# The head of an attention stage rearranged: clears, gate copies, a first sigmoid and the order of its loads

## The chip, the core and the metric

The kernel runs on one core of a Trainium2 chip. The metric is the device time of one execution in microseconds (us), lower is better. The core has five instruction queues that matter here, each working strictly in the order in which the program issues to it: PE (TensorE, matrix products), DVE (VectorE), ACT (ScalarE), POOL (GpSimd) and SP, which issues most of the loads. Some loads are issued from ACT's queue.

## What is computed

A gated linear attention over 4 batches, 8 heads, 768 positions of width 40, followed by two feed-forward layers: one in which 3072 tokens are routed to 8 experts, and one with a product of two projections. Only the first stage is touched by the change:

```python
for t in range(S):
    m_new = np.maximum(f_gate[:, :, t] + m, i_gate[:, :, t])
    f_stab = np.exp(f_gate[:, :, t] + m - m_new)
    i_stab = np.exp(i_gate[:, :, t] - m_new)
    m = m_new
    C = f_stab * C + i_stab * np.einsum('bhd,bhe->bhde', vt, kt)
    n = f_stab * n + i_stab * kt
    h_tilde = np.einsum('bhde,bhe->bhd', C, qt)
    denom = np.maximum(np.abs(np.einsum('bhd,bhd->bh', n, qt)), 1.0)
    o = 1.0 / (1.0 + np.exp(-o_gate[:, :, t]))
    y[:, :, t] = o * h_tilde / denom
```

(the indices that only broadcast are left out). All arithmetic is float32.

## The kernel before

The recurrence is computed in chunks of T = 128 positions. There are 6 chunks (`c`) and 4 batches (`b`), so 24 blocks, numbered `n = 4c + b`. All 8 heads of a block are worked on together.

**Per chunk**, `gates(c)` turns the gates of all batches and heads into exponents: a chain of small DVE operations on 128x128 tiles (a scan for the running maximum `mt`, then `lf`, `cc`, a second scan `A`, and `zs`), then three ACT operations (`hi`, and two parts of `EW`), then on DVE `ar` and `es1`, and from these the wide operands `mov` (8 heads, 128x1024) and `est` (4 batches, 128x512). `ar`, `es1` and `md` are small; `mov` and `est` are copies of `ar` and `es1` scaled by a 0/1 selector (`hsel`, `bsel`). For chunk 0 these copies are whole-tile multiplications, for later chunks they are twelve ACT copies spread through the blocks. `gates2(c)` transposes `EW` on PE (this needs the identity matrix `identf`) and brings the result to SBUF as `gt`.

**Per block**, `s1(n)` makes the weights `P` in two halves g: PE forms the exponents `pe` from `est` and `mov`, ACT takes `dd = exp(pe)`, POOL clears the upper triangle of `dd` (affine select), PE forms `pq` from `qr` (the loaded q and k), and DVE multiplies `P = pq * dd`. There is one `pe` buffer and there are two `pq` buffers. `s2(n)` multiplies by v on PE (`pv`, one buffer), updates the state (`pst`, `Cc`, `Cb`), and forms numerator `num` and denominator `den` on DVE. `xout(n)` multiplies `num` by 1/den and by the sigmoid of the output gate, `SG[c][:, b]`, on POOL, and stores the row. `s3` and `s4` feed the router.

**Buffers and loads.** `load(n)` issues five SP transfers: four of q and k into `qr[n % 3]` and one of v and k into `vk`. The `qr` tiles must be zero outside the loaded rows, so each of the three is cleared once before its first load. `load_o(c)` issues the transfer of the output gate (640 KB) from ACT's queue; `load_g(c)` that of the f and i gates (`fi`, 128 KB) from SP's.

**Order.** The schedule is written by hand: the program order of `attention` is the order of every queue. At the start: `consts` (POOL's `iota` of `jp`, then on DVE `identf` from it and the clear of `ones`), `load_g(0)` and the load of the selectors `gs`, the clears of `qr[0]`, `qr[2]`, `Cb` and two `xt` tiles on POOL and of `qr[1]` and `pst` on DVE, `load(0)`, `load(1)`, `load_o(0)`, then all of `gates(0)`, `load_g(1)`, `load_o(1)`, `gates2(0)`, `pre(0)`, `s1(0)`, then the clear and load of `wg`, and `consts2`. In `consts2` POOL's `iota` of `pcol` comes ahead of ACT's `thr`, which reads it, and DVE copies `thc` from `thr`. Then the loop over blocks runs: iteration `n` issues `load(n + 2)`, `s1(n + 1)` interleaved with `s2(n)`, and steps of a background generator (`fill`): from the start `gates(1)`, and from block 2 on the conversion of later weights. In iteration 0, behind the second half's matrix products of `s1(1)` and ahead of their DVE product `P`, stands `sig(0)`, the sigmoid of the first output gate: one ACT instruction over 128x1280 and a one-element exponential `warm` behind it. ACT holds the table of one set of functions at a time, and the profile shows a table load ahead of each of the two.

Of the kernel before, what the change touches and what calls it, by code (L numbers as in the profile page):

```python
# [14 lines left out]
AF = mybir.ActivationFunctionType  # L15
OP = mybir.AluOpType
# [4 lines left out]
B, H, S, D = 4, 8, 768, 40  # L21
T = 128
# [21 lines left out]
class Kern:  # L44
# [9 lines left out]
    def consts(self, es):  # L54
        nc, cp = self.nc, self.cp
        jp = self.jp = es.enter_context(self.tc.tile_pool(name="ajp", bufs=1)).tile([128, 128], F32, name="jp")
        nc.gpsimd.iota(jp, pattern=[[1, 128]], base=0, channel_multiplier=-1,
                       allow_small_or_imprecise_dtypes=True)
        self.identf = cp.tile([128, 128], F32, name="identf")
        nc.vector.tensor_scalar(self.identf, jp, 0.0, None, op0=OP.is_equal)  # L60
        self.spacer = cp.tile([1, 1], F32, name="spacer")
        self.ones = cp.tile([128, T], F32, name="ones")
        nc.vector.memset(self.ones, 1.0)

    def consts2(self):
        nc, cp, jp = self.nc, self.cp, self.jp
# [151 lines left out]
    def attention(self, es):  # L218
        tc, nc, a = self.tc, self.nc, self.a
# [9 lines left out]
        def load_g(c):  # L229
            t = ld.tile([128, 2, T], F32, name="fi", bufs=2)  # L230
            nc.sync.dma_start(t, a["fi4"][:, c])
            FI[c] = t
# [5 lines left out]
        hsel = gs[:, 6:14]  # L238
        dsel = gs[:, 14:30]
        psel = gs[:, 30:158]  # L240
        bsel = gs[:, 158:162]
# [3 lines left out]
        qr = [one.tile([128, 2 * H, T], F32, name=f"qr{i}") for i in range(NQ)]  # L245
        nc.gpsimd.memset(qr[0], 0.0)
        nc.vector.memset(qr[1], 0.0)
        nc.gpsimd.memset(qr[2], 0.0)
        Cb = one.tile([128, B, 4, 2, DE], F32, name="Cb")
        nc.gpsimd.memset(Cb, 0.0)  # L250
        Cc = one.tile([128, B, 4, DE], F32, name="Cc")
        xtb = [one.tile([128, 3, T], F32, name=f"xt{i}") for i in range(2)]
        for i in range(2):
            nc.gpsimd.memset(xtb[i][64:128, 2], 0.0)
        MT = {}
        pst = ps.tile([128, 4, DE], F32, name="pst")
        nc.vector.memset(pst, 0.0)
# [1 line left out]
        VK, SG, GA, PT, ST = {}, {}, {}, {}, {}  # L259

        def load(n):
            c, b = divmod(n, B)
            t = qr[n % NQ]
            bd = t[:, H:].rearrange("p (a s) t -> p a s t", s=2)
            for s in range(2):
                r, rs = slice(64 * s, 64 * s + D), slice(D * s, D * s + D)
                nc.sync.dma_start(t[r, 0:H], a["qk"][rs, c, b])
                nc.sync.dma_start(bd[r, :, s], a["qk"][rs, c, b, 0:4])
            v_ = ld.tile([128, H, DE + D], F32, name="vk")
            nc.sync.dma_start(v_, a["vk"][b, c])  # L270
            VK[n] = v_

        def load_o(c):
            o_ = ld.tile([128, B, DM], F32, name="og", bufs=2)
            SG[c] = o_
            self.dma(lambda: nc.scalar.dma_start(o_, a["og"][:, c]))

        def sig(c):
            nc.scalar.activation(SG[c], SG[c], AF.Sigmoid)
            nc.scalar.activation(warm, gs[0:1, 0:1], AF.Exp)  # L280

        def gates(c):
            t = FI.pop(c)
            fg, ig = t[:, 0], t[:, 1]
            mt = wk.tile([128, 1 + T], F32, name="mt")
            if c:
                nc.vector.tensor_copy(mt[:, 0:1], MT[c - 1][:, T:])
            else:
                nc.vector.memset(mt[:, 0:1], -1e30)
            MT[c] = mt  # L290
            mc, mp = mt[:, 1:], mt[:, 0:T]
            yield 0
            nc.vector.tensor_tensor_scan(mc, fg, ig, mp[:, 0:1], op0=OP.add, op1=OP.max)
            yield 0
            lf = wk.tile([128, T], F32, name="lf", bufs=1)
            nc.vector.tensor_add(lf, fg, mp)
            yield 0
            nc.vector.tensor_sub(lf, lf, mc)
            if c == 0:
                nc.vector.memset(lf[:, 0:1], 0.0)  # L300
            yield 0
            cc = wk.tile([128, T], F32, name="cc", bufs=1)
            nc.vector.tensor_sub(cc, ig, mc)
            A = wk.tile([128, T], F32, name="A", bufs=1)
            nc.vector.tensor_tensor_scan(A, self.ones, lf, 0.0, op0=OP.mult, op1=OP.add)
            yield 0
            zs = wk.tile([128, 2, T], F32, name="zs", bufs=1)
            nc.vector.tensor_scalar(zs[:, 1], A, za, oa, op0=OP.mult, op1=OP.add)
            nc.vector.tensor_sub(cc, cc, A)
            yield 0  # L310
            nc.vector.tensor_scalar(zs[:, 0], cc, zc, oc, op0=OP.mult, op1=OP.add)
            hi = wk.tile([128, 2, T], F32R, name="hi", bufs=1)
            EW = wk.tile([128, 2, T], F32, name="EW", bufs=1)

            def fin():
                nc.scalar.activation(hi, zs, AF.Copy)
                nc.scalar.activation(EW[:, 0], A, AF.Exp)
                nc.scalar.activation(EW[:, 1], cc, AF.Exp, bias=A[:, T - 1:T])

            yield from self.later(fin, False)  # L320
            ar = wk.tile([128, T], F32, name="ar", bufs=1)
            nc.vector.scalar_tensor_tensor(ar, hi[:, 1].bitcast(F32), b2, zs[:, 1], op0=OP.mult, op1=OP.add)
            mov = wk.tile([128, H, T], F32R, name="mov")

            def half(g):
                e = nc.vector if c == 0 and g else nc.gpsimd
                e.tensor_tensor(mov[:, 4 * g:4 * g + 4], ar[:, None, :].to_broadcast([128, 4, T]),
                                hsel[:, 4 * g:4 * g + 4, None].to_broadcast([128, 4, T]), op=OP.mult)

            if c == 0:  # L330
                half(0)
            es1 = wk.tile([128, T], F32, name="es1", bufs=1)
            nc.vector.scalar_tensor_tensor(es1, hi[:, 0].bitcast(F32), b1, zs[:, 0], op0=OP.mult, op1=OP.add)
            est = wk.tile([128, B, T], F32R, name="est")

            def spread(e, b0, b1_):
                e.tensor_tensor(est[:, b0:b1_], es1[:, None, :].to_broadcast([128, b1_ - b0, T]),
                                bsel[:, b0:b1_, None].to_broadcast([128, b1_ - b0, T]), op=OP.mult)

            if c == 0:  # L340
                spread(nc.vector, 0, 1)
            yield 0
            md = wk.tile([128, 16], F32, name="md", bufs=1)
            nc.vector.tensor_scalar(md, dsel, EW[:, 0, T - 1:T], None, op0=OP.mult)
            yield 0
            if c == 0:
                half(1)
                spread(nc.gpsimd, 1, B)
            else:
                def scaled(i0, i1):  # L350
                    for i in range(i0, i1):
                        if i < B:
                            nc.scalar.activation(est[:, i], es1, AF.Copy, scale=bsel[:, i:i + 1])
                        else:
                            nc.scalar.activation(mov[:, i - B], ar, AF.Copy, scale=hsel[:, i - B:i - B + 1])

                yield "w"
                for i in range(0, 12, 3):
                    scaled(i, i + 3)
                    yield "w"  # L360
            GA[c] = (est, mov, EW, md)
            yield 0
# [150 lines left out]
        def allof(g):  # L513
            for _ in g:
                pass

        NS = B * NC
        for n in range(2):
            load(n)
        load_o(0)  # L520
        self.hold = False
        allof(gates(0))
        load_g(1)
        load_o(1)
        gates2(0)
        pre(0)
        allof(s1(0))
        nc.vector.memset(wg, 0.0)
        nc.sync.dma_start(wg[:, 0:2, 0:E], a["moe_w_gate"][0:256, :].rearrange("(c p) e -> p c e", p=128))
        nc.sync.dma_start(wg[0:64, 2, 0:E], a["moe_w_gate"][256:320, :])  # L530
        self.consts2()
        self.hold = True
        bg.insert(0, gates(1))
        load_g(2)
        for n in range(NS):
            c, b = divmod(n, B)
            if n == 2:
                bg.append(m2)
            if True:
# [4 lines left out]
                if b == 3 and c + 1 < NC:  # L544
                    gates2(c + 1)
                    if c + 2 < NC:
                        bg.insert(0, gates(c + 2))
                        if c + 3 < NC:
                            load_g(c + 3)
                m = s1(n + 1) if n + 1 < NS else iter(())  # L550
                next(m, None)
                g = s2g(n)
# [4 lines left out]
                if n == 0:  # L557
                    sig(0)
                if b == 3 and c + 1 < NC:
                    sig(c + 1)  # L560
# [6 lines left out]
                g = s2(n)  # L567
# [662 lines left out]
```

## Time and profile before

| | us |
|---|---|
| median of 3 runs | 909.09 |
| lowest and highest of these | 905.57, 910.00 |
| the profiled execution, its own time | 908.33 |
| its span in the profile | 906.6 |
| PE busy | 822.6 |
| DVE busy | 538.4 |
| POOL busy | 415.9 |
| ACT busy | 353.3 |

The profiled execution lies 0.76 us under the median, and its span 1.7 us under its own time. Mean granted clock of TensorE in it: 0.955 of full speed. The attention takes the first 200 us or so of the span, the routing and the two feed-forward layers the rest. A row of a timeline gives start, duration, engine, line, operation, output and inputs with their shapes, and in brackets the idle time of the engine before it with what ended it.

### The profile page before, as it was taken

Reading aid. Unit: us, or ns where it says so; the run is one execution under the profiler, and the core shown is the slowest. Engines: PE = TensorE matmul, PEld = TensorE weight load, DVE = VectorE, ACT = ScalarE, POOL = GpSimd, SP = SyncE. Lnnn points to the kernel's source line nnn. Section 1 sums busy time; section 2 is a strip of 40 time slices with the busy share of each in tenths; the row PEclk is TensorE's granted clock in tenths of the full one; section 3 lists DMA queues with packets and bytes.
Section 4 is the critical chain, followed back from the end, with each engine's and each line's share of the span. In section 5 each row is a group of like instructions: output and inputs, shape, how many; then the busy total and the mean of one; then the engine's idle time right before and its main releaser. Section 6 shows DMA issues by size and latency. Waiting matters only on the chain.

```text
span 906.6 us, 15898 instructions
## 1 busy us (share of the span) xinstructions
PE 822.6 (91%) x5939; PEld 780.7 (86%) x5939; DVE 538.4 (59%) x1188; ACT 353.3 (39%) x720; POOL 415.9 (46%) x441
## 2 busy tenths in 40 slices
PE   4889889976888799989989999999999999999996
PEld 3778788875777799979879998999899999999996
DVE  7678898756866974776576687476764212311211
ACT  4778777610443332232233234224322532532321
POOL 5577787621513670464056338233723823532122
PEclk9999999995889989979989999999999999999999
DMA  6877777413122310220120122031111301200000
GB/s 169 245 230 213 234 214 228 136 59 104 52 67 81 89 59 9 76 75 22 54 80 18 37 78 59 1 97 48 30 53 45 105 24 44 76 1 23 1 1 22
DMA packets 51037, 73.84 MB, mean 81 GB/s; under 512 B 6160, under 2 KB 41360, under 8 KB 50960
## 3 DMA queue, kind: packets, MB, share of 16 engines
q1 hardware_dynamic: 41744, 45.30, 17.7%
q10 hardware_dynamic: 6912, 19.66, 6.6%
q0 software_dynamic: 2304, 7.87, 2.7%
q8 instruction: 47, 0.77, 0.4%
q14 instruction: 30, 0.25, 0.1%
HBM read 63.37 MB, written 7.86 MB: 79 GB/s over the span
## 4 chain that ended last, share of the span: by engine, by line
PE 66%; DVE 15%; ACT 7%; issue 4%; DMA 4%; POOL 2%; SPq 0%; ACTq 0%; DVEq 0%; POOLq 0%
PE ring L983 33%; PE acc L983 20%; DVE G L661 4%; PE pq L405 2%; PE rt L685 2%; PE pv L436 2%; DVE w1h L920 1%; DMA qr<-in_qk_dram 1%; PE pl L495 1%; DMA vk<-in_vk_dram 1%; DVE gf L1106 1%; PE pe L397 1%; PE pg L421 1%; DMA mraw<-in_wab_dram 1%; ACT yh L979 1%
## 5 line engine op out<-in xcount | busy, mean ns | idle before, releaser
L1111 POOL TENSOR_TENSOR ml<-gf,mh 128x384 fp32r<-128x384 f32 x95 | 106.5, 1121 | 267.3 <-ACT mh L1108 266.8
L983 PE MATMUL ring<-yh,wh 128*128 128x384 f32 x576 | 203.5, 353 | 6.6 <-ACT yh L979 4.6
L983 PE MATMUL ring<-yl,wh 128*128 128x384 f32 x576 | 137.5, 345 | 0.0
L983 PE MATMUL ring<-yh,wl 128*128 128x384 f32 x384 | 133.7, 348 | 0.0
L1106 DVE TENSOR_TENSOR gf<-ring,at 128x384 f32<-128x384 f32 x96 | 53.3, 555 | 129.1 <-PE ring L983 125.0
L983 PEld LDWEIGHTS ring<-yh,wh 128*128 128x128 f32 x576 | 112.6, 196 | 14.1 <-ACT yh L979 7.2
L1108 ACT ACTIVATE mh<-gf 128x384 fp32r<-128x384 f32 x96 | 50.4, 525 | 189.7 <-DVE gf L1106 189.7
L661 DVE TENSOR_TENSOR G<-thc,d 128x1024 bf16<-128x1024 int16 (+1 forms) x90 | 109.6, 1236 | 0.4
L983 PEld LDWEIGHTS ring<-yl,wh 128*128 128x128 f32 x576 | 106.2, 194 | 0.0
L983 PE MATMUL acc<-woh,ml 128*128 128x320 f32 x288 | 91.5, 318 | 0.0
L983 PE MATMUL acc<-woh,mh 128*128 128x320 f32 x288 | 90.6, 315 | 0.0
L983 PE MATMUL acc<-wol,mh 128*128 128x320 f32 x288 | 90.4, 314 | 0.0
L983 PE MATMUL acc<-mh,w 128*128 128x384 f32 x320 | 88.4, 339 | 0.0
L1049 DVE SCALAR_TENSOR_TENSOR ml<-ring,mh 128x384 fp32r<-128x384 f32 x64 | 35.5, 556 | 80.3 <-ACT mh L1047 77.7
L1047 ACT ACTIVATE mh<-ring 128x384 fp32r<-128x384 f32 x64 | 31.4, 491 | 132.8 <-PE ring L983 126.8
L1104 ACT ACTIVATE at<-ring 128x384 f32<-128x384 f32 x96 | 46.8, 487 | 78.6 <-PE ring L983 76.8
L983 PEld LDWEIGHTS ring<-yh,wl 128*128 128x128 f32 x384 | 75.1, 195 | 0.0
L919 POOL TENSOR_TENSOR w1l<-raw,w1h 128x512 fp32r<-128x512 f32 x30 | 44.0, 1472 | 51.2 <-ACT w1h L915 51.2
L983 PE MATMUL ring<-xh,w1h 128*128 128x384 f32 x192 | 65.6, 342 | 0.1
L983 PE MATMUL acc<-ml,w 128*128 128x384 f32 x192 | 64.8, 338 | 0.8 <-DVE ml L1049 0.8
L983 PEld LDWEIGHTS acc<-mh,w 128*128 128x128 f32 x320 | 58.5, 189 | 0.2 <-issue 0.2
L983 PEld LDWEIGHTS acc<-woh,mh 128*128 128x128 f32 x288 | 55.1, 191 | 2.6 <-issue 2.6
(213 smaller groups left out, 1726.7 us busy)
## 6 DMA issues: line engine op xcount, KB each, us to landing
raw<-in_moe_w_dram SPq DMA_DIRECT2D x32, 320.0 KB
raw<-in_moe_w_dram SPq DMA_DIRECT2D x32, 256.0 KB
vk<-in_vk_dram SPq DMA_DIRECT2D x24, 324.0 KB
qr<-in_qk_dram SPq DMA_DIRECT2D x48, 160.0 KB
mraw<-in_wab_dram ACTq DMA_DIRECT2D x12, 640.0 KB
raw<-in_moe_w_dram SPq DMA_DIRECT2D x64, 64.0 KB
og<-in_og_dram ACTq DMA_DIRECT2D x6, 640.0 KB
qr<-in_qk_dram SPq DMA_DIRECT2D x48, 80.0 KB
```

The lines of the kernel that those rows point to most:

```text
L405: nc.tensor.matmul(pq[:, o:o + 2], qk[:, 4 + hp], qk[:, H + 2 * hp:H + 2 * hp + 2], start=True, stop=True)
L436: nc.tensor.matmul(pvf[:, 64 * h:64 * h + w], P[:, h], vkf[:, (DE + D) * h:(DE + D) * h + w], start=True, stop=True)
L661: self.nc.vector.tensor_tensor(G, self.thc[:, None, 0:nthr].to_broadcast(dims), d[:, i0:i0 + 8, None].to_broadcast(dims), op=op)
L685: nc.tensor.matmul(cnt[0:nthr], Gs[j][:, i], oh[:, 8 * j + i], start=(j + i == 0), stop=(j * 8 + i == NT - 1))
L919: e.tensor_sub(l, raw[:, 0:2], h[:, 0:2].bitcast(F32))
L983: self.nc.tensor.matmul(*a, **k)
L1047: A.activation(hh, p, AF.Relu)
L1049: V.scalar_tensor_tensor(hl, p, 0.0, hh.bitcast(F32), op0=OP.max, op1=OP.subtract)
L1104: A.activation(at, p[0], AF.Copy)
L1106: V.tensor_mul(gf, p[1], at)
L1108: A.activation(gh, gf, AF.Copy)
L1111: e.tensor_sub(gl, gf, gh.bitcast(F32))
```

## The change

It touches only the start of `attention` and what belongs to it.

- `identf` is formed in `gates(0)` behind the last `zs`, instead of ahead of DVE's clears.
- The clears of `qr[2]`, `Cb` and the two `xt` tiles on POOL move from the start to behind `s1(0)`, which is ahead of `consts2`.
- `load(1)` and `load_o(0)` are issued behind `gates(0)`. On SP this changes nothing in the order, since `gates(0)` issues nothing there. On ACT's queue the transfer of the first output gate now stands behind ACT's work for `gates(0)`.
- The gate copies of chunk 0: before, POOL made the first half of `mov`, DVE the first of four parts of `est`, then `md`, then the second half of `mov`, and POOL the other three parts of `est`. Now ACT makes the first part of `est`, DVE the first half of `mov` and then `md`, POOL the second half of `mov` and the other parts of `est`.
- `sig(0)` becomes an exponential of the negated gate on ACT, an addition of 1 on POOL (128x1280), and four reciprocals on DVE (128x320 each). The sigmoid, its `warm` and both table loads go away for this chunk; the later chunks keep them.

```diff
     def consts(self, es):
         self.identf = cp.tile([128, 128], F32, name="identf")
-        nc.vector.tensor_scalar(self.identf, jp, 0.0, None, op0=OP.is_equal)
         ...
+    def ident(self):
+        self.nc.vector.tensor_scalar(self.identf, self.jp, 0.0, None, op0=OP.is_equal)
         ...
         nc.gpsimd.memset(qr[0], 0.0)
         nc.vector.memset(qr[1], 0.0)
-        nc.gpsimd.memset(qr[2], 0.0)
-        nc.gpsimd.memset(Cb, 0.0)
-        for i in range(2):
-            nc.gpsimd.memset(xtb[i][64:128, 2], 0.0)
         ...
         def sig(c):
+            if c == 0:
+                nc.scalar.activation(SG[c], SG[c], AF.Exp, scale=-1.0)
+                nc.gpsimd.tensor_scalar(SG[c], SG[c], 1.0, None, op0=OP.add)
+                for b in range(B):
+                    nc.vector.reciprocal(SG[c][:, b], SG[c][:, b])
+                return
             nc.scalar.activation(SG[c], SG[c], AF.Sigmoid)
             nc.scalar.activation(warm, gs[0:1, 0:1], AF.Exp)
         ...
             nc.vector.tensor_scalar(zs[:, 0], cc, zc, oc, op0=OP.mult, op1=OP.add)
+            if c == 0:
+                self.ident()
         ...
             def half(g):
-                e = nc.vector if c == 0 and g else nc.gpsimd
+                e = nc.gpsimd
         ...
-            if c == 0:
-                half(0)
         ...
             if c == 0:
-                spread(nc.vector, 0, 1)
+                scaled(0, 1)
+                nc.vector.tensor_tensor(mov[:, 0:4], ar[:, None, :].to_broadcast([128, 4, T]),
+                                        hsel[:, 0:4, None].to_broadcast([128, 4, T]), op=OP.mult)
         ...
-        for n in range(2):
-            load(n)
-        load_o(0)
+        load(0)
         self.hold = False
         allof(gates(0))
+        load(1)
+        load_o(0)
         load_g(1)
         load_o(1)
         gates2(0)
         pre(0)
         allof(s1(0))
+        nc.gpsimd.memset(qr[2], 0.0)
+        nc.gpsimd.memset(Cb, 0.0)
+        for i in range(2):
+            nc.gpsimd.memset(xtb[i][64:128, 2], 0.0)
         nc.vector.memset(wg, 0.0)
```

`scaled(i0, i1)` are the ACT copies that later chunks already use; it only moved up in the text.

## Rows read from the trace of the kernel before

**Rows 1.** The page: busy time of PE; the chain that ended last, by engine
```profile
PE   822.6 (91%) x5939; PEld 780.7 (86%) x5939; DVE 538.4 (59%) x1188; ACT 353.3 (39%) x720; POOL 415.9 (46%) x441
PE 66%; DVE 15%; ACT 7%; issue 4%; DMA 4%; POOL 2%; SPq 0%; ACTq 0%; DVEq 0%; POOLq 0%
```

**Rows 2.** Timeline of DVE, 0 to 10 us: start, duration, operation [idle, releaser]
```profile
1.20 4.67 DVE L60 TENSOR_SCALAR identf<-jp 128x128 f32<-128x128 f32 x1 [1.20 <-POOL jp L57]
4.11 1.76 DVE L247 MEMSET qr<- 128x2048 f32 x1
6.19 0.48 DVE L293 TENSOR_TENSOR_SCAN mt<-fi,mt 128x128 f32<-128x128 f32 x1
...
9.44 0.35 DVE L322 SCALAR_TENSOR_TENSOR ar<-hi,gs,zs 128x128 f32<-128x128 f32 x1 [0.48 <-ACT hi L316]
```

**Rows 3.** Timeline of POOL and of SP's queue, the first 7 us
```profile
2.86 1.79 POOL L248 MEMSET qr<- 128x2048 f32 x1
4.61 1.18 POOL L250 MEMSET Cb<- 128x1312 f32 x1
5.84 0.35 POOL L254 MEMSET xt<- 64x128 f32 x2
...
2.94 0.37 SPq L267 DMA_DIRECT2D qr<-in_qk_dram  x1
```

**Rows 4.** DMA queues, 0 to 3 us (q10 is ACT's): packets, MB, share
```profile
q10 hardware_dynamic: 25, 0.13, 37.2%
q1 hardware_dynamic: 13, 0.01, 1.8%
```

**Rows 5.** Chain that ended last, 0 to 60 us: start, duration, what
```profile
3.69 4.86 DMA qr<-in_qk_dram
```

**Rows 6.** Timelines of POOL, DVE and PE around the gate copies of chunk 0
```profile
9.94 1.04 POOL L327 TENSOR_TENSOR mov<-ar,gs 128x512 fp32r<-128x512 f32 x1 [3.75 <-issue]
...
10.09 1.04 DVE L337 TENSOR_TENSOR est<-es,gs 128x128 fp32r<-128x128 f32 x1
11.05 0.79 DVE L344 TENSOR_SCALAR md<-gs,EW 128x16 f32<-128x16 f32 x1
11.76 0.68 DVE L327 TENSOR_TENSOR mov<-ar,gs 128x512 fp32r<-128x512 f32 x1
...
12.35 0.77 PE L397 MATMUL pe<-mov,est 128*128 128x512 f32 x1
```

**Rows 7.** Timelines of POOL and ACT between the first and the second block
```profile
15.96 0.63 POOL L400 TENSOR_SCALAR_AFFINE_SELECT dd<-dd 128x512 f32<-128x512 f32 x1 [1.49 <-ACT dd L399]
...
16.72 1.15 ACT L74 ACTIVATE thr<-jp,pcol 128x1024 int16<-128x1024 f32 x1 [0.83 <-POOL pcol L71]
17.78 0.58 ACT L399 ACTIVATE dd<-pe 128x512 f32<-128x512 f32 x1
```

**Rows 8.** Timelines of ACT, DVE and PE from the first sigmoid to chunk 1's copies
```profile
20.85 1.27 ACT L279 ACTIVATE og<-og 128x1280 f32<-128x1280 f32 x1
...
19.62 1.35 DVE L408 TENSOR_TENSOR P<-pq,dd 128x512 f32<-128x512 f32 x2
...
23.43 0.34 DVE L311 TENSOR_SCALAR zs<-cc,gs 128x128 f32<-128x128 f32 x1
...
25.08 1.10 PE L405 MATMUL pq<-qr 128*128 128x256 f32 x4 [2.71 <-DMA qr<-in_qk_dram]
...
30.26 1.28 ACT L353 ACTIVATE est<-es,gs 128x128 fp32r<-128x128 f32 x4 [1.28 <-DVE es L333]
```

**Rows 9.** DVE's three 8-element operations, by line: ns min/median/max of one
```profile
L465 DVE RECIPROCAL den<-den x24: 186/195/204, 23.3 to 192.4; 128x8 f32<-128x8 f32 x24
...
L450 DVE TENSOR_SCALAR den<-num x24: 137/374/830, 22.5 to 192.0; 128x8 f32<-128x8 f32 x24
...
L463 DVE SCALAR_TENSOR_TENSOR den<-num,den x24: 149/422/639, 22.8 to 192.2; 128x8 f32<-128x8 f32 x24
```

**Rows 10.** Groups of DVE by line and form, 0 to 205 us: busy, mean ns
```profile
L445 DVE TENSOR_TENSOR num<-num,pv 128x328 f32<-128x328 f32 x20 | 9.8, 488 | 4.6 <-PE pv L436 4.4
```

More of the change, by code (lines that the diff above doesn't have):

```diff
@@ L338, in spread, with scaled @@
                                 bsel[:, b0:b1_, None].to_broadcast([128, b1_ - b0, T]), op=OP.mult)
+            def scaled(i0, i1):
+                for i in range(i0, i1):
+                    if i < B:
+                        nc.scalar.activation(est[:, i], es1, AF.Copy, scale=bsel[:, i:i + 1])
+                    else:
+                        nc.scalar.activation(mov[:, i - B], ar, AF.Copy, scale=hsel[:, i - B:i - B + 1])
             if c == 0:
-                spread(nc.vector, 0, 1)
+                scaled(0, 1)
+                nc.vector.tensor_tensor(mov[:, 0:4], ar[:, None, :].to_broadcast([128, 4, T]),
+                                        hsel[:, 0:4, None].to_broadcast([128, 4, T]), op=OP.mult)
             yield 0
@@ L349, in gates @@
             else:
[L350 to L355, printed above, removed]
                 yield "w"
```

## Prediction

> **What bounds the kernel now.** I read the page first: PE is busy for nine tenths of the span and carries two thirds of the chain that ended last [rows 1]. The change touches none of the products that fill this chain; it touches the first 30 us, in which PE has little to do and the five queues wait for one another. Time that this head gains or loses is passed on: from the loop's start to the end of the attention the transfers are issued when buffers come free, so a delay of the head delays them too, and the later stages start when the attention ends. So I read the head in the timelines, engine by engine.
>
> On DVE the reader is to see that the first scan of the gates starts at 6.19, behind `identf`, which took 4.67 us beside POOL's clears, and the clear of `qr[1]` [rows 2]. The rest of DVE's short clears took from 4.11 + 1.76 = 5.87 to 6.19, 0.32 us. On POOL the clears of `qr[2]`, `Cb` and `xt` fill the time to 6.19 [rows 3], in which nobody needs POOL. That is the idle cover they have now. The DMA rows show that ACT's queue, with the output gate, had moved 0.13 MB by 3.0 us and SP's, with the gates that the scan needs, 0.01 MB [rows 4].
>
> **The change, part by part.** All times are on the clock of the run before; what is gained up to a point is taken off at the end.
>
> *Start of the scan.* DVE without `identf` needs 1.76 + 0.32 = 2.08 us for its clears, starting between 0 and the 1.20 at which it started before [rows 2]: ready between 2.1 and 3.3. The f and i gates are 0.13 MB, just what ACT's queue had moved by 3.0 us [rows 4], and it no longer stands ahead. No row shows their landing; bounds are 3.0 and 4.0, since the latter leaves a further microsecond for the selectors and the signal. I take 3.4, nearest to the rate of that row: 6.19 - 3.4 = **2.8 us gained** (2.2 to 3.2). `load(0)` is issued at 2.94 as before [rows 3], its third transfer landed at 8.55 [rows 5], now without the output gate ahead of it. Its first reader stands behind `pe`, now at 12.35 - 2.3 = 10.0 [rows 6]: hidden, with 1.5 us to spare. SP's queue passes nothing, as `gates(0)` issues nothing there. `load_o(0)` moves behind `gates(0)` on ACT's queue; its 640 KB are read at about 23 below, so it is hidden, and would cost only what it lands later than that.
>
> *`identf` behind `zs`.* It falls into DVE's 0.48 us wait for `hi` [rows 2], POOL now being idle. Nothing; up to 0.3 us if it reaches out of that wait.
>
> *The copies of chunk 0.* DVE's copy of `est`, 128 columns, took 1.04 us and ended 0.15 us behind POOL's product, while the half of `mov`, four times as large, took 0.68 us once POOL was done; `md`, 16 columns, took 0.79 us beside POOL's next product [rows 6]. So a DVE product waits for the POOL product beside it. After the change POOL starts its half of `mov` as soon as `ar` is there, at 9.94 as now, until 10.98; DVE's half follows, to about 11.5; then POOL's three parts of `est` run and `md`, which stands behind DVE's half, ends near 12.3, not at 11.84. PE's first `pe` waits behind the product with `md`. I take **0.5 us lost**. If DVE gets in first, `md` ends at about 10.1 + 0.7 + 0.2 = 11.0, a gain of 0.8. Up to here the net gain is 2.8 - 0.5 = 2.3.
>
> *The clears behind `s1(0)`.* POOL's last select of block 0 ends at 15.96 + 0.63 = 16.59 [rows 7]. Now 1.79 + 1.18 + 0.35 = 3.3 us of clears follow [rows 3], and behind them the `iota` of `pcol`, on which ACT's `thr` waits. In ACT's queue `dd` of block 1 stands behind `thr` [rows 7]. So `thr` starts at 16.72 + 3.3 = 20.0 and ends at 21.2, and `dd` runs from 21.2 to 21.8, not from 17.78. DVE's queue stops at the same place, since `thc` reads `thr`. `load(2)` waits for `qr[2]` until 16.6 + 1.8 = 18.4 and was issued later than that anyway: nothing. Taken alone the 3.3 us would be mostly covered, as PE stood for 2.71 us until 25.08 for the q of block 2 [rows 8].
>
> *The first sigmoid.* With one `pe` buffer, the second `pe` and `dd` of block 1 follow: 0.5 + 0.6 and two hand-overs, to 23.0. The exponential has the sigmoid's shape, 1.27 us [rows 8]: 24.3. The two table loads and `warm` that go away lay in a time in which PE waited for q, so no gain is booked. The addition on POOL over 1280 columns has no row of its own: by the clear (1.79 us for 2048 [rows 3]) 1.1 us, by the select (0.63 for 512 [rows 7]) 1.6, by the product (1.04 for 512 [rows 6]) 2.6. The select is the nearest, an operation with one input: 1.6, to **25.9**. DVE waits for it with four reciprocals at the head of its queue, and behind these are queued the second `P` of block 1, the whole of `num` and `den` of block 0, and the chain of `gates(1)`.
>
> What a reciprocal over 320 columns takes is the term that decides. The trace has only 8 columns: 186 to 204 ns, 195 in the median, where the quickest 8-column operations of the two other kinds took 137 and 149 [rows 9]. If that excess of 37 (186 - 149) to 58 ns (195 - 137) is a fixed cost, 320 columns cost what 328 cost in an addition, 0.49 us [rows 10], and four 2.0. If it is paid per column, it is 4.6 to 7.25 ns each, and 320 columns cost 0.49 + 1.5 to 0.49 + 2.3, that is 2.0 to 2.8 us, and four 7.9 to 11.2. I take the second reading, 2.5 us each and **10.0 us** for four: the reciprocal is the steadiest of the three kinds and yet never came down to the others' time, and an excess of a fixed cost alone has no neighbour in the rows that shows one.
>
> The Trainium skill ("VectorE: DVE Perf Modes", The DVE is not a fixed-function vector unit) says that Reciprocal runs as an iterative divide with a repeat count of 8. Read as eight cycles of the 0.96 GHz that the page gives, 320 columns would be 2.7 us, by estimate, four 10.7, and the time 0.7 us above mine; no row of more than 8 columns shows it, and those of 8 do not contradict it.
>
> So DVE is free at 25.9 + 10.0 = 35.9. From the second `P` of block 1 to the end of `zs` it took, before, from 20.3 to 23.77, 3.5 us without a stop [rows 8]: 39.4. Two `P` of block 2 take 1.35 [rows 8]: 40.75; `ar` (0.35 [rows 2]) and `es1` 0.65: 41.4. Then ACT can start on `est` of chunk 1, which it did at 30.26, having waited for just this [rows 8]. That is 11.2 us later; less the 2.3, **8.9 us lost**. From there the order of work is the old one and I find no wait that gives the loss back. The sum against the profiled execution's own time: 908.33 + 8.9 = **917.2**. (That execution lies 0.8 under the median of the runs.)
>
> **The rivals.** *Cheap reciprocals.* If the excess is a fixed cost, the four take 2.0, DVE is free at 27.9, `est` starts at 33.4, 3.1 late, less 2.3: 0.8 lost, **909.1**, with bounds 906.9 (addition 1.1, scan at 3.0, copies -0.8) and 910.8. For it speaks that 46 ns could be the length of another program; against it that no other operation of this size stands so apart and so steady. This is also the rival on the other side: not slower. It decides from about 0.8 us a reciprocal downwards.
>
> *The loss is absorbed.* While DVE stands, ACT and SP run ahead, and the transfers of blocks 3 and 4 and the first weights are there when the loop moves again; the waits for transfers in the next blocks, of the size of the 2.71 us [rows 8], vanish. Two of them give 4 to 5 us back: **912.8**. Against it: the buffers, not the transfers, hold the loads back.
>
> *The head's gain stays whole.* If `thr` does not hold `dd` back and all the new work fits into the waits up to 25.08, the 2.3 us are left: **906.0**. Against it stands the order of POOL's and ACT's queues.
>
> **How the numbers follow.** Forecast 0.64, absorbed 0.08, cheap reciprocals 0.23, gain whole 0.05. The forecast alone spans 914 to 920.5 (reciprocals 7.9 to 11.2, addition 1.1 to 2.6, scan 3.0 to 4.0). For 8 in 10 the range must take in half of the cheap case: 908.8 to 921. A measurement of this kernel can tell about 0.5%, 4.5 us, from no change. Slower by more: nearly all of the forecast and a part of the absorbed case, 0.64. Within: 0.32. Faster by more needs a gain larger than the whole head offers: 0.04.
>
> **What would show it.** Right: the scan near 3.4; `thr` starting behind the clears, about 20.0 - 2.3 = 17.7; four reciprocals in a row on DVE of 2 to 2.8 us each, ending near 33.6, with PE idle or nearly so beside them; `est` of chunk 1 near 39. Wrong: reciprocals of half a microsecond; `dd` of block 1 not behind `thr`; the gap in PE's row in front of block 1's `pv` closed again by 60 us.

## Result: slower by about one per cent

| | before | after |
|---|---|---|
| median, us (4 runs each) | 909.55 | 920.28 |
| lowest to highest, us | 905.57 to 910.38 | 916.15 to 921.39 |
| ratio of the times | | 1.0117 (1.0082 to 1.0152) |
| the profiled execution, its own time and its span, us | 908.33, 906.6 | 916.15, 914.4 |

A later repetition of both gave a ratio of 1.0094 (1.0062 to 1.0127). The changed kernel is slower by 8.5 to 10.6 us. The profiled execution of the changed kernel is the fastest of its four, so that the two profiled executions differ by only 7.8 us. Its page, beside [rows 1]: the line with the busy times, and the chain that ended last.

```profile
PE 820.9 (90%) x5939; PEld 778.3 (85%) x5939; DVE 548.5 (60%) x1191; ACT 350.9 (38%) x718; POOL 422.6 (46%) x442
...
PE 64%; DVE 17%; ACT 8%; issue 5%; DMA 3%; POOL 2%; ACTq 0%; DVEq 0%; POOLq 0%; SPq 0%
```

DVE has 10 us more of work (538.4 before), 8.4 us of it the four new reciprocals, and its share of the chain grew from 15% to 17%. The rest of this section follows the head in time.

**The gates' chain and the copies.** DVE's timeline, to compare with [rows 2] and [rows 6]:

```profile
3.46 0.06 DVE L293 MEMSET mt<- 128x1 f32 x1
3.55 0.48 DVE L297 TENSOR_TENSOR_SCAN mt<-fi,mt 128x128 f32<-128x128 f32 x1
...
6.23 0.22 DVE L65 TENSOR_SCALAR identf<-jp 128x128 f32<-128x128 f32 x1
...
7.33 1.53 DVE L353 TENSOR_TENSOR mov<-ar,gs 128x512 fp32r<-128x512 f32 x1
...
8.78 0.79 DVE L357 TENSOR_SCALAR md<-gs,EW 128x16 f32<-128x16 f32 x1
```

The scan starts at 3.55 instead of 6.19, right behind the last of DVE's clears. `identf`, which took 4.67 us, takes 0.22 in its new place. DVE's half of `mov` takes 1.53 us beside POOL's product, and `md` ends at 9.57, which is 6.02 behind the start of the scan, where it was 11.84 - 6.19 = 5.65: the copies lost 0.4 us.

**The clears.** POOL and ACT behind the first block, to compare with [rows 7]:

```profile
14.27 1.81 POOL L534 MEMSET qr<- 128x2048 f32 x1
...
17.86 1.15 ACT L76 ACTIVATE thr<-jp,pcol 128x1024 int16<-128x1024 f32 x1 [4.23 <-POOL pcol L73]
...
18.91 0.58 ACT L405 ACTIVATE dd<-pe 128x512 f32<-128x512 f32 x1
```

`thr` starts behind the clears, at 17.86, and the first `dd` of block 1 behind it at 18.91, later than in the kernel before (17.78) although all before it ran 2.3 us earlier.

**A wait nobody had planned.** SP's queue in the middle of `load(1)`; SP's waits in the first 20 us (in total, times, longest); and the chain that ended last, from 7.87 to 19.70:

```profile
4.98 0.30 SPq L265 DMA_DIRECT2D qr<-in_qk_dram  x1
...
12.63 0.28 SPq L266 DMA_DIRECT2D qr<-in_qk_dram  x1
```

```profile
SPq L266 <- DMA og<-in_og_dram: 8.5, 2, 7.3
```

```profile
7.87 6.57 DMA og<-in_og_dram
...
14.46 3.07 DMA qr<-in_qk_dram
...
17.66 2.04 PE pq L411 x4
```

SP waited twice in the middle of `load(1)`: 7.3 us ahead of its second transfer, until the first output gate had landed, and 1.2 us ahead of its fourth, until the second gate, issued by `load_o(1)` at 7.87, had landed at 14.44. So PE had the q of block 1 only at 17.66. The trace shows what ties the queues together: each transfer of SP's and ACT's queues reports its landing on one of eight semaphores (counters that an instruction can wait for). The second and fourth transfers of `load(1)` use those of the two output gates, and SP waited for just these before it issued them, at 12.63 and 14.46. The product then ended at 19.70, just behind the `dd` of 18.91 to 19.49, so it was this load, by a hair, and not the clears, that ended last ahead of the second `pe` and `dd` of block 1.

**The new sigmoid.** ACT's exponential, POOL's addition, DVE's reciprocals and the first `P` behind them, PE's first product behind that, and ACT's `dd` and `est`:

```profile
20.87 1.26 ACT L278 ACTIVATE og<-og 128x1280 f32<-128x1280 f32 x1
...
22.21 3.46 POOL L279 TENSOR_SCALAR og<-og 128x1280 f32<-128x1280 f32 x1 [0.54 <-ACT og L278]
...
25.71 8.19 DVE L281 RECIPROCAL og<-og 128x320 f32<-128x320 f32 x4 [4.61 <-POOL og L279]
...
33.81 0.63 DVE L414 TENSOR_TENSOR P<-pq,dd 128x512 f32<-128x512 f32 x1
...
34.50 2.07 PE L411 MATMUL pq<-qr 128*128 128x256 f32 x4 [9.28 <-DVE P L414]
...
34.56 0.60 ACT L405 ACTIVATE dd<-pe 128x512 f32<-128x512 f32 x1 [9.89 <-DVE P L414]
...
40.06 1.28 ACT L347 ACTIVATE est<-es,gs 128x128 fp32r<-128x128 f32 x4 [0.97 <-DVE es L337]
```

Addition and reciprocals run one behind the other from 22.21 to 33.90, and the second `P` of block 1 stands behind them. PE waits 9.28 us for it, ACT 9.89. `est` of chunk 1 starts at **40.06** instead of 30.26 [rows 8]: 9.8 us later. The windows of 5 us show what this does to PE (length; busy time of PE, its weight loads, DVE, ACT and POOL, with the instructions; granted clock; share and GB/s of the DMA engines):

```profile
25.00:30.00 5.00, 0.22 (x1) 0.00 (x0) 4.29 (x3) 0.00 (x0) 2.71 (x4) 0.75 0.63 170
...
30.00:35.00 5.00, 0.50 (x1) 0.50 (x2) 4.96 (x6) 0.44 (x1) 0.00 (x0) 0.50 0.02 7
```

PE and ACT do nearly nothing from 25 to 34 us, and TensorE's granted clock falls to 0.50, 1.2 instead of 2.4 GHz, after PE has stood still.

### The profile page after: what moved, and what is told of

Its sections match the earlier page's. It is cut to its first block, busy times and chain, and to the rows that moved or that the text cites. A ratio compares the mean times of both kernels' runs of the same rounds, so it can differ in the third digit from the quotient of the medians.

```text
span 914.4 us, 15900 instructions
## 1 busy us (share of the span) xinstructions
PE 820.9 (90%) x5939; PEld 778.3 (85%) x5939; DVE 548.5 (60%) x1191; ACT 350.9 (38%) x718; POOL 422.6 (46%) x442
## 3 DMA queue, kind: packets, MB, share of 16 engines
q0 software_dynamic: 2304, 7.87, 2.7%
## 4 chain that ended last, share of the span: by engine, by line
PE 64%; DVE 17%; ACT 8%; issue 5%; DMA 3%; POOL 2%; ACTq 0%; DVEq 0%; POOLq 0%; SPq 0%
PE ring L993 32%; PE acc L993 20%; DVE G L671 4%; PE rt L695 2%; PE pq L411 2%; PE pv L442 2%; DVE w1h L930 1%; DVE gf L1116 1%; ACT mq L194 1%; DVE og L281 1%; DMA mraw<-in_wab_dram 1%; PE pg L427 1%; PE pl L501 1%; ACT yh L989 1%; PE pe L403 1%
## 5 line engine op out<-in xcount | busy, mean ns | idle before, releaser
L411 PE MATMUL pq<-qr 128*128 128x256 f32 x192 | 54.6, 411 | 13.5 <-DVE P L414 10.4
```

The source lines that it names most:

```text
L411: nc.tensor.matmul(pq[:, o:o + 2], qk[:, 4 + hp], qk[:, H + 2 * hp:H + 2 * hp + 2], start=True, stop=True)
```

## The experiments

Each row of the table at the end of this section gives a run's ratio to the kernel before, measured on the same chip at the same time. One per cent is 9.1 us.

**The old sigmoid in the changed kernel.**

```diff
 def sig(c):
-    if c == 0:
-        ...  (exponential, addition, four reciprocals)
     nc.scalar.activation(SG[c], SG[c], AF.Sigmoid)
```

> The changed kernel with its first sigmoid put back to one sigmoid instruction with its two table loads and the one-element exponential; everything else as changed. Theory (the addition on POOL and the reciprocals on DVE hold the queue): ACT is free of the sigmoid at about 25.1 us, DVE's second P of block 1 starts near 21.7 instead of 33.8, est of chunk 1 on ACT starts near 30 instead of 40.1, as in the kernel before (30.3), and the time is that of the kernel before, ratio 1.000, 908 to 911 us. Rival (the clears ahead of pcol, thr and dd are the cost): dd of block 1 stays at 18.9 and the loss stays with it, est not before 33, at least 913 us, ratio 1.004 or more.

Measured: ratio 0.9989 (0.9961 to 1.0016). DVE's second `P` of block 1, and ACT's `est`:

```profile
22.15 0.69 DVE L408 TENSOR_TENSOR P<-pq,dd 128x512 f32<-128x512 f32 x1 [1.05 <-PE pq L405]
...
30.55 1.28 ACT L341 ACTIVATE est<-es,gs 128x128 fp32r<-128x128 f32 x4 [1.27 <-DVE es L331]
```

`P` comes at 22.15, not 33.81, and `est` 0.3 us behind the kernel before. The loss goes with the new sigmoid, to within the 2.5 us of the interval, though the first `dd` of block 1 is still at 18.91. The rival that blames the clears falls.

**The new sigmoid alone, in the kernel before.**

> The kernel before with the new first sigmoid alone (exponential on ACT, addition on POOL, four reciprocals on DVE). Theory: the exponential runs from 19.6 to 20.8, the addition takes 3.5 us to 24.3, the reciprocals 8.2 us to 32.6, and est of chunk 1 starts 6.2 us behind them at 38.8 instead of 30.3: 8.5 us lost, 918 us, ratio 1.009. Rival (the clears are the cost): without the moved clears the new operations fit into the waits up to 25 us, 909 to 911 us, ratio 1.000 to 1.002.

Measured: ratio 1.0063 (1.0038 to 1.0087), 3.5 to 7.9 us lost. POOL's addition, DVE's reciprocals, ACT's `est`:

```profile
20.80 3.46 POOL L281 TENSOR_SCALAR og<-og 128x1280 f32<-128x1280 f32 x1 [0.54 <-ACT og L280]
...
24.29 8.19 DVE L283 RECIPROCAL og<-og 128x320 f32<-128x320 f32 x4 [4.00 <-POOL og L281]
...
38.65 1.28 ACT L359 ACTIVATE est<-es,gs 128x128 fp32r<-128x128 f32 x4 [0.97 <-DVE es L339]
```

The steps of the head came as expected, `est` at 38.65 against 38.8. Slower, as the theory said, but by less: its ratio of 1.009 lies just outside the interval. In the head the loss is 8.4 us against the trace of before, 7.1 against the control below, whose own `est` came 1.3 us later; only the first of these is more than the 7.9 at which the interval ends.

**One reciprocal instead of four.**

```diff
-for b in range(B):
-    nc.vector.reciprocal(SG[c][:, b], SG[c][:, b])
+nc.vector.reciprocal(SG[c], SG[c])
```

> The changed kernel with one reciprocal over 1280 columns instead of four over 320. Theory (a price per column, 8.19 us for the four): one instruction of 8.0 to 8.4 us, the time as changed, 919 to 921 us, ratio 1.011. Rival (a price per instruction, 2.1 us each): one instruction of 2.1 to 3 us, 5 to 6 us less, 914 us, ratio 1.005.

Measured: ratio 1.0110 (1.0082 to 1.0138), and one instruction of

```profile
25.69 8.15 DVE L280 RECIPROCAL og<-og 128x1280 f32<-128x1280 f32 x1 [4.61 <-POOL og L279]
```

So the price is per column. With 0.195 us for 8 columns [rows 9] and 8.15 for 1280: (8.15 - 0.195) / 1272 = 6.25 ns a column and a fixed part of 0.15 us, which gives 2.15 for 320, where the four in the changed kernel had a median of 2.10.

**The addition on DVE.**

```diff
-nc.gpsimd.tensor_scalar(SG[c], SG[c], 1.0, None, op0=OP.add)
+nc.vector.tensor_scalar(SG[c], SG[c], 1.0, None, op0=OP.add)
```

> The changed kernel with the addition of 1 over 128x1280 on DVE instead of POOL. Theory (POOL's 3.46 us are its own speed and stand in the chain): DVE needs 0.8 to 1.4 us, the reciprocals start 2.1 to 2.7 us earlier, 917.8 us, ratio 1.009. Rival (the addition took so long because it waited for something, and that wait stays): no more than 0.5 us less, 920 us, ratio 1.0115.

Measured: ratio 1.0054 (1.0027 to 1.0081). DVE's addition, and `est` on ACT:

```profile
21.85 1.66 DVE L279 TENSOR_SCALAR og<-og 128x1280 f32<-128x1280 f32 x1 [0.77 <-ACT og L278]
...
37.87 1.28 ACT L347 ACTIVATE est<-es,gs 128x128 fp32r<-128x128 f32 x4 [0.97 <-DVE es L337]
```

1.66 us on DVE, beside POOL's `wv` and a clear and longer than the 0.8 to 1.4 expected, against 3.46 on POOL, where DVE stood idle: POOL's time is its own speed. `est` comes 2.2 us earlier than in the changed kernel. The time fell by more than that (0.6% between the two ratios), but the two intervals all but meet, and the one of the second control overlaps; why it fell by more is not shown.

**The clears in front, with the old sigmoid.** POOL's clears are back at the start; the three edits left are `identf`, the copies and the order of the loads.

> The changed kernel with the old first sigmoid and with POOL's clears of qr[2], Cb and xt back at the start; what stays of the change is identf behind zs, the copies of chunk 0 on three engines, and load(1) and load_o(0) behind the gates' chain. Theory: the scan still starts near 3.5, since the clears of POOL run beside scans and not beside identf; thr starts at 14.5 instead of 17.9 and the first dd of block 1 at 15.6 instead of 18.9, but PE's pq of block 1 waits for its q until 16 to 17.7 as before, because SP's second transfer of load(1) waits for the transfer of the output gate, so the second dd of block 1 gains only 0.5 to 1.5 us: ratio 0.997 to 1.000. Rival (the load does not matter): second dd 2.5 to 3 us earlier than 20.4, est of chunk 1 near 27.7, ratio 0.996. Second rival: the clears slow the gates' chain beside them and hi starts 1 us or more later than 6.35, ratio 1.000 or more.

Measured: ratio 0.9963 (0.9931 to 0.9996). DVE's half of `mov` and `md`; ACT's `hi`, `thr` and second `dd` of block 1:

```profile
7.33 0.68 DVE L351 TENSOR_TENSOR mov<-ar,gs 128x512 fp32r<-128x512 f32 x1
...
7.93 1.01 DVE L355 TENSOR_SCALAR md<-gs,EW 128x16 f32<-128x16 f32 x1
...
6.35 0.42 ACT L320 ACTIVATE hi<-zs 128x256 fp32r<-128x256 f32 x1 [4.24 <-DVE zs L313]
...
13.82 1.15 ACT L76 ACTIVATE thr<-jp,pcol 128x1024 int16<-128x1024 f32 x1 [0.83 <-POOL pcol L73]
...
19.25 0.60 ACT L403 ACTIVATE dd<-pe 128x512 f32<-128x512 f32 x1 [3.81 <-PE pe L401]
```

From the scan, at 3.55 again, to `hi` it takes 2.80 us, with POOL's clears beside it until 6.19. It took 2.80 in the changed kernel, where POOL was idle, and 2.80 before (6.19 to 8.99). So the clears never held this chain; only `identf` had waited for them. `thr` is back at 13.82, yet the second `dd` comes at 19.25, only 1.1 us earlier: PE waited 2.26 us for the q of block 1, until 16.75, as the theory said. In the time the theory's 0.997 and the rival's 0.996 can't be told apart. In this run DVE's half of `mov` went ahead of POOL's (0.68 us instead of 1.53) and `md` ended at 8.94, 0.6 us earlier than in the changed kernel; the two start within 0.1 us of each other, and which goes first differs between kernels with the same copies.

**The output gate loaded behind the rest,** on top of the last kernel.

```diff
+    e = nc.sync if c < 2 else nc.scalar
-    self.dma(lambda: nc.scalar.dma_start(o_, a["og"][:, c]))
+    self.dma(lambda: e.dma_start(o_, a["og"][:, c]))
 ...
 load(1)
-load_o(0)
 load_g(1)
+load_o(0)
 load_o(1)
```

> The kernel of the run with the clears in front, and the transfers of the first two output gates issued from SP's queue behind load(1) and the next f and i gates, instead of from ACT's. Theory: SP no longer waits in the middle of load(1), the q of block 1 is there by 10 to 12 us, pq of block 1 follows its pe without a wait near 14.3, the second dd of block 1 runs near 17.0, and est of chunk 1 starts near 28 instead of 30.3, 2.3 us before the kernel before: ratio 0.9975. Rival (q was not what held block 1): the same time as the run with the clears in front.

Measured: ratio 0.9969 (0.9938 to 0.9999). PE's first product of q and k of block 1, and of block 2; ACT's second `dd` of block 1 and `est`:

```profile
13.81 1.02 PE L410 MATMUL pq<-qr 128*128 128x256 f32 x4
...
21.88 1.10 PE L410 MATMUL pq<-qr 128*128 128x256 f32 x4 [2.42 <-DMA qr<-in_qk_dram]
...
16.03 0.60 ACT L404 ACTIVATE dd<-pe 128x512 f32<-128x512 f32 x1 [0.59 <-PE pe L402]
...
27.07 1.28 ACT L346 ACTIVATE est<-es,gs 128x128 fp32r<-128x128 f32 x4 [1.09 <-DVE es L336]
```

`load(1)` goes through without a wait for an output gate, PE does not wait for the q of block 1, its second `dd` is 3.2 us earlier than with the load in the way, and `est` is at 27.07, 3.2 us ahead of the kernel before. In the time it can't be told from the run before. The next wait shows already: the q of block 2.

**The loads of the router and of chunk 2's gates behind `load(2)`,** on top of the last kernel.

> The kernel of the run with the gate loads behind, and on SP's queue the loads of the router's weights and of the f and i gates of chunk 2 moved behind load(2). Theory: load(2) no longer waits for DVE's clear of wg and goes out near 9.4 us instead of 16.6; PE's wait of 2.4 us for the q of block 2 at 21.9 goes, est of chunk 1 starts 0.5 to 1.5 us earlier than 27.1, near 26: ratio 0.9955 against the kernel before, 1 us under the run with the gate loads behind. Rival (ACT's sigmoid with its table loads, until 20.6, holds the second half of block 2 anyway): est at 27, ratio 0.997.

Measured: ratio 0.9968 (0.9932 to 1.0005). PE's first product of q and k of block 2, and ACT's `est`:

```profile
19.31 1.02 PE L410 MATMUL pq<-qr 128*128 128x256 f32 x4
...
25.60 1.28 ACT L346 ACTIVATE est<-es,gs 128x128 fp32r<-128x128 f32 x4 [1.14 <-DVE es L336]
```

PE's wait for the q of block 2 is gone and `est` starts at 25.60, 4.7 us ahead of the kernel before and 1.5 ahead of the last run, the most that was expected. The time did not visibly follow: the ratio is that of the two runs before, though its interval holds the expected 0.9955 too.

**The reciprocals where their results are read,** in the changed kernel.

```diff
-for b in range(B):
-    nc.vector.reciprocal(SG[c][:, b], SG[c][:, b])
 ...  (in xout, ahead of the product with the gate)
+if c == 0:
+    nc.vector.reciprocal(SG[c][:, b], SG[c][:, b])
```

> The changed kernel with each of the four reciprocals of the first output gate moved from the head of DVE's queue to the place where its result is first read, ahead of the block's product with the gate, one in each of blocks 0 to 3; the exponential and the addition stay where they are. Theory (it is the place in DVE's queue that costs, with P, num and the gates of chunk 1 behind the reciprocals): no operation of the loop waits for the addition any more, est of chunk 1 starts near 30 as with the old sigmoid, and of the 8.2 us of reciprocals 0 to 4 us remain, in blocks 1 to 4: ratio 0.998 to 1.004. Rival (their length costs wherever they stand, DVE being the bound): 6 to 8 us remain, ratio 1.007 to 1.009.

Measured: ratio 1.0061 (1.0030 to 1.0092). DVE's `lf` of chunk 1 beside POOL's addition, the first reciprocal, POOL's product that waits for it, PE's transposes behind the second such product, and `est`:

```profile
22.75 2.62 DVE L298 TENSOR_TENSOR lf<-fi,mt 128x128 f32<-128x128 f32 x1
...
31.69 2.10 DVE L480 RECIPROCAL og<-og 128x320 f32<-128x320 f32 x1
...
33.93 1.18 POOL L481 TENSOR_TENSOR x<-x,og 128x320 f32<-128x320 f32 x1 [3.87 <-DVE og L480]
...
44.13 0.55 PE L491 MATMUL px<-identf,x 128*128 128x128 f32 x3 [3.12 <-POOL x L481]
...
30.51 1.28 ACT L345 ACTIVATE est<-es,gs 128x128 fp32r<-128x128 f32 x4 [0.72 <-DVE es L335]
```

`est` is back at 30.51, so the queue no longer stands; but the shift of the blocks (table below) then grows from -1.2 us at block 2 to 6.4 at block 5. The time decides between neither side: 5.5 us stayed, and the interval, 2.7 to 8.4, reaches into the theory's 0 to 4 and holds the rival's 6 to 8; the trace, with 6.4 at block 5, is nearer to the rival. The new places are not idle ones: POOL's product waits for each reciprocal, and PE's transposes of its result stand in PE's queue in the middle of the next block's products with v. Nor is DVE free of the addition: `lf` took 2.62 us beside it, where it took 0.28 from the same 22.75 on in the run with the old sigmoid.

**The sigmoid by a hyperbolic tangent,** in the kernel before.

```diff
-nc.scalar.activation(SG[c], SG[c], AF.Sigmoid)
-nc.scalar.activation(warm, gs[0:1, 0:1], AF.Exp)
+nc.scalar.activation(SG[c], SG[c], AF.Tanh, scale=0.5)
+nc.scalar.activation(SG[c], SG[c], AF.Copy, bias=1.0)
 ...  (den doubled: max(x, 1) * 2, then max(-2x, den))
```

> The kernel before with every sigmoid computed from a hyperbolic tangent: tanh of half the gate and an addition of 1, both on ACT over 128x1280, with the factor of a half taken into the denominator, where it costs no instruction. Theory: no table load is left but the first (each 1.28 us, twelve of them go away), six one-element exponentials go, six additions of 1.27 us come, and no operation is added to DVE or POOL: 9 us less of ACT in the attention; where ACT's sigmoid stood in front of a dd that PE waits for, some of it is gained, 0 to 1.5 us a chunk, 904 to 910 us on the earlier scale, ratio 0.994 to 1.000. Rival: ACT has slack at all six places and nothing is gained, ratio 1.000.

Measured: ratio 1.0015 (0.9988 to 1.0043): 0.1% gained at most. That is what the rival said, that ACT has slack in these places. No table load but the first is left in the trace.

**Both: the clears on ACT and the tangent,** on top of the kernel with the output gate loaded behind.

> Head of the changed kernel with its costs taken out: POOL's clears of qr[2], Cb and xt made by ACT in its idle time from 2.1 to 6.3 us (copies scaled by 0), the output gates of chunks 0 and 1 loaded from SP's queue behind load(1) and the next f and i gates, and all sigmoids by the hyperbolic tangent. Theory: scan near 3.5, hi near 6.35 or up to 0.5 later if the clears reach into it, second dd of block 1 near 17, est of chunk 1 near 26.5 to 28, 2.5 us before the kernel before, and the gain of the tangent in the later chunks on top: ratio 0.991 to 0.9975. Rival: the gain of the head is lost at the next wait for a load, ratio as for the tangent alone.

Measured: ratio 0.9993 (0.9960 to 1.0025). The largest of ACT's clears, its second `dd` of block 1 and `est`; PE's first product of block 2:

```profile
2.12 1.91 ACT L255 ACTIVATE qr<-ones 128x2048 f32<-128x2048 f32 x1
...
16.67 0.60 ACT L408 ACTIVATE dd<-pe 128x512 f32<-128x512 f32 x1 [0.59 <-PE pe L406]
...
29.08 1.28 ACT L350 ACTIVATE est<-es,gs 128x128 fp32r<-128x128 f32 x4 [1.28 <-DVE es L340]
...
22.75 2.04 PE L414 MATMUL pq<-qr 128*128 128x256 f32 x4 [2.65 <-DMA qr<-in_qk_dram]
```

Half of the expectation came: the clears fit ACT's idle time and the second `dd` is at 16.67. Then PE waited 2.65 us for the q of block 2, the product behind that wait ran at half its speed (2.04 us, where the kernel with the output gate loaded behind had 1.10), and `est` came at 29.08, only 1.2 us early. The rival has it in the head; in the time the interval also reaches the theory's 0.9975.

**Control: both kernels unchanged, once more, on one chip.**

> The kernel before once more, unchanged, as a control for the shifts along the blocks. Theory (the head is the same every time, and what differs behind block 10 is from execution to execution): its first 30 us as in the trace of before within 0.1 us, est of chunk 1 at 30.3, and its later blocks off that trace by up to several us, as they were with the old sigmoid in the changed kernel (0.3 us at block 5, 9.3 us at block 18). Rival (those late shifts came from the edits): every block within 1 us of the trace of before.

> The changed kernel once more, unchanged, beside the control. Theory: est of chunk 1 at 40.1 as before, 9.8 us behind the control's, that shift kept through block 10, and behind it differences of several us to either side of 9.8; ratio of the times 1.009 to 1.014. Rival (a part of the loss is given back behind the head): a ratio under 1.007.

Measured: ratios 0.9990 (0.9963 to 1.0016) and 1.0094 (1.0062 to 1.0127). In the kernel before, PE's first product of block 2 and ACT's `est`; the window of PE's slow stretch, and the same window in the trace of before:

```profile
25.27 2.05 PE L405 MATMUL pq<-qr 128*128 128x256 f32 x4 [2.91 <-DMA qr<-in_qk_dram]
...
31.59 1.28 ACT L353 ACTIVATE est<-es,gs 128x128 fp32r<-128x128 f32 x4 [1.31 <-DVE es L333]
```

```profile
25.00:30.00 5.00, 4.73 (x13) 3.95 (x14) 1.13 (x2) 1.91 (x6) 1.55 (x3) 0.50 0.82 214
...
25.00:30.00 5.00, 4.92 (x44) 4.54 (x45) 2.86 (x4) 2.19 (x6) 2.81 (x4) 1.00 0.97 253
```

The expectation of a head that repeats within 0.1 us missed. PE waited 2.91 us for the q of block 2, where it had waited 2.71 [rows 8], and the product behind the wait took 2.05 us instead of 1.10, at a granted clock of 0.50. `est` came at 31.59, 1.3 us later, in the same program. The changed kernel had it at 40.04, 8.45 behind this control, and the loss is 0.94%, 8.5 us, as the theory of a loss that is kept has it; the interval, from 1.0062 on, still reaches the rival's side of 1.007.

**All runs.** Start of `est` of chunk 1 on ACT; start of the `pst` products of blocks 5, 10 and 18 less that in the trace of before (57.54, 96.25, 158.38); and the ratio, turned into us by 909.55. The shifts are of one execution each, on several chips; the kernel before had medians from 909.4 to 913.2 us on them.

| kernel | est | block 5 | block 10 | block 18 | ratio as us (interval) |
|---|---|---|---|---|---|
| before | 30.26 | 0 | 0 | 0 | 0 |
| before, control | 31.59 | +0.6 | +2.7 | +3.8 | -0.9 (-3.4 to 1.5) |
| after | 40.06 | +9.0 | +9.5 | +10.7 | +10.6 (7.5 to 13.8) |
| after, control | 40.04 | +8.8 | +10.2 | +14.5 | +8.5 (5.6 to 11.6) |
| old sigmoid | 30.55 | +0.4 | +1.1 | +9.3 | -1.0 (-3.5 to 1.5) |
| new sigmoid alone | 38.65 | +7.6 | +8.8 | +11.6 | +5.7 (3.5 to 7.9) |
| one reciprocal | 40.00 | +8.7 | +10.2 | +14.6 | +10.0 (7.5 to 12.6) |
| addition on DVE | 37.87 | +6.8 | +9.1 | +13.8 | +4.9 (2.5 to 7.4) |
| clears in front | 29.25 | -1.0 | +2.5 | +5.5 | -3.4 (-6.3 to -0.4) |
| gate load behind | 27.07 | -1.4 | +2.6 | +3.3 | -2.8 (-5.6 to -0.1) |
| router load last | 25.60 | -5.0 | -3.9 | -0.2 | -2.9 (-6.2 to 0.5) |
| reciprocals spread | 30.51 | +6.4 | +6.0 | +14.2 | +5.5 (2.7 to 8.4) |
| tangent | 31.79 | +0.4 | +0.9 | +3.5 | +1.4 (-1.1 to 3.9) |
| both | 29.08 | -2.5 | -2.4 | -1.6 | -0.6 (-3.6 to 2.3) |

Up to block 5 the shift is that of `est`, within about 2 us, but for the spread reciprocals, which come behind `est`. Behind block 10 single executions part by several us, the control too, and kernels that are alike by block 5 part by more (old sigmoid and tangent: +9.3 and +3.5 at block 18). There ACT's queue stops for transfers in some executions and not in others. ACT's longest waits for transfers from 50 to 200 us, in the kernel with the old sigmoid and in the second control (in total, times, longest):

```profile
ACT Cb L460 <- DMA wh<-mth: 4.6, 1, 4.6
```

```profile
ACT Cb L466 <- DMA xd<-x: 5.1, 2, 2.7
```

The traces of before and of the tangent have no wait of ACT for a transfer in this stretch, so these waits are not the only cause. Which transfer is late in which execution was not taken apart, and so it stays open why the 4.7 us of the best head end as 3, if they do: the interval holds both. The three kernels without the new sigmoid that keep the early scan and the clears in front are the fastest measured; two of their three intervals end below one, by 0.04% and 0.01%, so that a gain is barely shown for them.

## Why the prediction was right, point by point

The time, 920.28, lies in the range, 0.7 us under its upper end, and the sign and the size are those forecast (8.9 us; measured 8.5 to 10.6). The forecast of 917.2 started from the profiled execution, 1.2 us under the median of before, and the upper bounds that it names (reciprocals 11.2, addition 2.6, scan 4.0) add up to 920.0 and not to the 920.5 given. By its steps:

- **Start of the scan**: 3.55, forecast 3.4, though not by the wait that set the 3.4. The text had DVE ready between 2.1 and 3.3 and the gates' landing as the later; the scan followed DVE's last clear, which ended at 3.52, and the trace has the gates landed at 2.92. `identf` cost nothing in its new place, as forecast.
- **The copies**: 0.4 us lost, forecast 0.5, in the way described, DVE's product held beside POOL's. The other end, DVE first, is not hypothetical: the run with the clears in front showed it.
- **The clears**: first `dd` of block 1 at 18.91, forecast 21.2 - 2.3 = 18.9.
- **The loads: failed.** The text called `load_o(0)` behind `gates(0)` hidden, and looked only at when its data are read. It did not ask who else waits for that transfer: SP's queue did, for 7.3 us, in the middle of `load(1)`, and 1.2 us more for the gate of `load_o(1)`. So the second `dd` of block 1 ended where the text had it (20.97, forecast 20.7), but behind the load and not behind the clears. It cost little only because the clears had already made block 1 late: with the clears back in front the wait still held the second `dd` at 19.25, and without it that `dd` came at 16.03.
- **The addition: mis-sized.** 3.46 us against 1.6, outside the bounds of 1.1 to 2.6. The select was the wrong neighbour; at 2.7 ns a column POOL's addition of a constant is slower than its product of two tiles (2.0 ns by [rows 6]).
- **The reciprocals: the deciding term, right in kind.** The excess over other 8-column operations is paid per column, and the four took 8.19 us, forecast 10.0 (7.9 to 11.2). The cheap rival, 909.1, falls with the single reciprocal. The Trainium skill ("VectorE: DVE Perf Modes", "First, the fixed hardware budget") says that Reciprocal uses iterative-divide operations with a repeat count of 8. Read as eight cycles a column, that gave 10.7 us in the prediction's estimate; the measured 6.25 ns a column are, by estimate, 6.0 cycles of the 0.96 GHz that the Trainium skill gives ("VectorE: DVE Perf Modes", "Specifications"). The measurement decides: six and not eight.
- **From the reciprocals to `est`**: 33.90 to 40.06, 6.2 us, forecast 5.5. In sum `est` came at 40.06, forecast 41.4 - 2.3 = 39.1: the addition 1.9 too short and the reciprocals 1.8 too long cancel, so the good total is in part luck.
- **Absorbed**: the changed kernel and its control kept the whole of it (9.8 and 8.45 us in the head, 10.6 and 8.5 in the time). The new sigmoid alone and the addition on DVE have less in the time (5.7 and 4.9) than in the head: 8.4 and 7.6 against the trace of before, with intervals that end at 7.9 and 7.4, but 7.1 and 6.3 against the control, which these intervals hold. So no run shows that a part is given back, and none rules out a few microseconds.

## What to carry to other kernels

A cheap-looking element-wise operation has to be priced per column, from two sizes, before it is put in front of a queue that others wait behind: the reciprocal that cost 0.2 us on 8 columns cost 8.2 on 1280, which is three times the two table loads (2.6 us) that it was to save, and those had lain in a wait. When a transfer is moved, ask not only when its data are read but which queue stops until it has landed. And a clear that moves out of one chain's way must not land ahead of the small operation that the next chain waits for, even if no run here shows that cost in the time; in front it had been in nobody's way but that of one instruction, `identf`. Moving only that one is the cheaper change to try; no run here did it by itself.

## What the hardware showed beyond the forecast

- DVE's reciprocal: 0.195 us for 8 columns, 2.10 for 320, 8.15 for 1280, 6.25 ns a column.
- The same addition of a constant to 128x1280: 3.46 us on POOL, 1.66 on DVE.
- POOL's clears did not slow DVE's scans and sums beside them (2.80 us from scan to `hi` with and without them), while `identf` beside the clears took 4.67 us and alone 0.22, and `tri`, an operation of the same kind, 1.92 beside the moved clears and 0.16 without.
- DVE's half of `mov` took 1.53 us beside POOL's product, against 0.68 where it went first, and `lf` 2.62 us beside POOL's addition, against 0.28 without.
- The landing of the transfers of SP's and ACT's queues is told by eight semaphores in all; a small load whose semaphore was that of a 640 KB transfer was issued 7.3 us late, when that had landed.
- TensorE's clock after a wait: in two executions of one program PE waited 2.71 and 2.91 us until 25.08 and 25.27, and the granted clock from 25 to 30 us was 1.00 in the first and 0.50 in the second, where `est` came 1.3 us later.
